# The opening of a fused attention and two-layer kernel: softmax sums of units 0 and 1 in column tiles, spread by transfers and multiplied by GpSimd

## The chip, the cores and the metric

The kernel runs on one core of a Trainium2 chip. The metric is the device time of one execution in microseconds (us). Before the change the median of three runs is 421.29 us (421.18 to 422.32). Engines are named as in the profile: PE is TensorE (matmuls; PEld are its weight loads), DVE is VectorE, ACT is ScalarE, POOL is GpSimd, SP is SyncE, which here only issues transfers. "L214" is line 214 of the kernel. Times of single events are counted from the start of the profiled span.

## The reference, cut to what matters

```python
def _attn_ref(q, k, v, g_q, g_k):             # q, k, v: (8, 12, 448, 64) float32
    q_n, k_n = rmsnorm(q, g_q), rmsnorm(k, g_k)
    scores = 1/sqrt(64) * q_n @ k_n.T
    attn = exp(scores - max(scores))           # rows of 448 keys
    attn = attn / (sum(attn) + 1e-09)
    return attn @ v

x = attention output as (3584, 768)
h = x @ moe_w_in                               # 768 x 2048
g = maximum(0.01 * h, h)
out = g @ moe_w_out                            # 2048 x 768
```

The kernel cuts the attention into 24 units: a unit is four heads of one batch, so a batch is three units. When the three units of a batch are done, the batch's x is complete and goes through the two weight matrices.

## The kernel before: the parts that the change touches

A unit has q and k as tiles of 128 partitions by 2 x 448 numbers. Its life is: square (`prep_sq` on ACT or `prep_sqp` on POOL), sum of squares (`prep_ssq`, DVE), inverse root (`prep_rinv`, ACT), normalise to f16 (`prep_norm`, DVE), transpose into `qkT` (PE plus a copy), scores in seven steps `qk` (PE), a row maximum for the shift (`shift_max`, `shift_mm`: DVE, PE, DVE), seven exponentials `ex` (ACT, one of 128x896 for each step), then the sums and the product with v.

There are two ways to form the sums and divide by them. The wide one is used by units 0 to 3 and the last one:

```python
def zsum(u, t0=0, t1=NS):                     # every sum stands 64 times: one row per row of the product
    for t in range(t0, t1):
        for r in range(2):
            for a in range(2):
                nc.tensor.matmul(s["zt"][r][64 * a:64 * a + 64, 0:S], ones16[64 * r:64 * r + 64],
                                 s["et"][64 * r:64 * r + 64, t, a], start=(t == 0), stop=(t == NS - 1))
def zinv(u):                                  # 1/z = exp(-ln z), read from PSUM
    s["rz"] = zpool.tile([P, 2, S], FP32, tag="rz", name="rz")
    nc.scalar.activation(s["rz"], s["zslot"][:, :, 0:S], AF.Ln)
    nc.scalar.activation(s["rz"], s["rz"], AF.Exp, bias=0.0, scale=-1.0)
def xmul(u):                                  # DVE multiplies the product in PSUM
    for r in range(2):
        nc.vector.tensor_tensor(xts[b][:, g, r], s["pv"][r][:, 0:S], s["rz"][:, r], op=ALU.mult)
```

The narrow one is used by units 4 to 22 (`narrow(u)` is `4 <= u < NU - 1`). The sums stand in four column tiles of 32 rows, only 224 columns wide; ACT takes the logarithm and the inverse of that small tile, and four transfers on the SP queue repeat it over the 128 partitions. The product is copied out of PSUM and multiplied from on-chip memory:

```python
def zcol(u):
    s["zc"] = aux([P, 512], FP32, "zc")
    for t in range(NS):
        for y in range(2):
            for a in range(2):
                c = 32 * (2 * y + a)
                nc.tensor.matmul(s["zc"][c:c + 32, 0:HS], onesr, s["et"][:, t, a, HS * y:HS * y + HS], ...)
def pv_out(u):
    s["x32"] = zpool.tile([P, 2, S], FP32, tag="x32", name="x32")
    nc.scalar.copy(s["x32"], s["pslot"][:, :, 0:S])
def zcol_ln(u):
    s["zs"] = zpool.tile([P, HS], FP32, tag="zs", name="zs")
    nc.scalar.activation(s["zs"], s["zc"][:, 0:HS], AF.Ln)
def zcol_inv(u):
    nc.scalar.activation(s["zs"], s["zs"], AF.Exp, bias=0.0, scale=-1.0)
    s["rz"] = zpool.tile([P, 2, S], FP32, tag="rz", name="rz")
    for r in range(2):
        for y in range(2):
            src = s["zs"][64 * y + r:64 * y + 64:2, None, :]
            nc.sync.dma_start(s["rz"][:, r, HS * y:HS * y + HS], src.broadcast_to([32, 4, HS]))
def xmul_pool(u, eng=nc.gpsimd):
    eng.tensor_tensor(xts[b][:, g], s["x32"], s["rz"], op=ALU.mult)
```

The pools that these tiles come from:

```python
raws  = tile_pool(name="raws",  bufs=3)      # q and k as loaded
zpool = tile_pool(name="zpool", bufs=1)      # x32, zs, rz: one buffer each, for all units
psum: tag "sT" bufs=2 (slot(), two banks each), tag "aux" bufs=4 (one bank each)
```

The weights come in on the POOL queue while the first units are at work: `load_w_in` is eight transfers, `load_w_out` two, and each v tile (`load_v`) one. q and k are loaded on the SP queue (`load`). [...] The end of the opening, up to the steady loop:

```python
ex(2)                                        # step 6 of unit 2
prep_rinv(4)
sums(2, 4, 5)
qk(3, STEPS[0])
sums(2, 5, NS)
zinv(2)                                      # unit 2 stays wide
shift_max(3)
xmul(2)
push(0)
first = slot()
moe1_part(0, first, 0, KT - 2)               # first matmuls of batch 0: parts 0, 1 of x are unit 0, parts 2, 3 unit 1
shift_mm(3)
ex(3)
moe1_part(0, first, KT - 2, KT - 1)          # part 4: unit 2
moe1_part(0, first, KT - 1, KT)              # part 5: unit 2
```

The `warm(n, bank)` calls are n matmuls whose result nobody reads; they keep PE active.

Of the kernel before, what the change touches and what calls it, by code (L numbers as in the profile page):

```python
# [8 lines left out]
FP32 = mybir.dt.float32  # L9
# [9 lines left out]
def kernel(  # L19
# [114 lines left out]
    def buf(u, name):  # L134
        if name not in st[u]:
            shape, dtype, bufs = SHAPES[name]
            st[u][name] = prep_p.tile(shape, dtype, tag=name[:2] if bufs == 3 and name != "qkT" else name, bufs=bufs, name=name)
        return st[u][name]
# [7 lines left out]
    def prep_sqp(u, tis=BOTH):  # L146
        for ti in tis:
            nc.gpsimd.tensor_tensor(buf(u, f"sq{ti}"), raw[u][ti], raw[u][ti], op=ALU.mult)
# [4 lines left out]
    def prep_ssq(u, c=ALL, tis=BOTH):  # L153
        for ti in tis:
            nc.vector.tensor_reduce(buf(u, "ssq")[:, ti, :, c[0]:c[1]], buf(u, f"sq{ti}")[:, :, c[0]:c[1]],  # L155
                                    axis=AXL.X, op=ALU.add)

    def prep_rinv(u, tis=BOTH):
        x = slice(tis[0], tis[-1] + 1)
        nc.scalar.activation(buf(u, "uu")[:, x], buf(u, "ssq")[:, x], AF.Ln, bias=eps_t, scale=1.0 / D)  # L160
        nc.scalar.activation(buf(u, "rinv")[:, x], buf(u, "uu")[:, x], AF.Exp, bias=0.0, scale=-0.5)  # L161
# [36 lines left out]
    def qk(u, steps):  # L198
        st[u]["sT"] = []
        for t in steps:  # L200
            sT = slot()
            score(u, t, (sT[:, 0], sT[:, 1]))
            st[u]["sT"].append((t, sT))

    def ex(u):
        s = st[u]
        if "et" not in s:
            s["et"] = epool.tile([P, NS, 2, S], FP16, tag="et", name="et")
        for t, sT in s["sT"]:
            if isinstance(sT, list):  # L210
                for a in range(2):
                    nc.scalar.activation(s["et"][:, t, a], sT[a][:, 0:S], AF.Exp, bias=s["eb"], scale=1.0)
            else:
                nc.scalar.activation(s["et"][:, t], sT[:, :, 0:S], AF.Exp, bias=s["eb"], scale=1.0)  # L214
# [6 lines left out]
    def shift_max(u):  # L221
        s = st[u]
        sT = s["sT"][0][1]
        if isinstance(sT, list):
            pm2 = small.tile([P, 2], FP32, tag="pm2", name="pm2")
            for a in range(2):
                nc.vector.tensor_reduce(pm2[:, a:a + 1], sT[a][:, 0:S], axis=AXL.X, op=ALU.max)
            s["spare"] = sT[0]
            nc.vector.tensor_reduce(s["spare"][:, 511:512], pm2, axis=AXL.X, op=ALU.max)
        else:  # L230
            s["spare"] = sT[:, 0]
            nc.vector.tensor_reduce(s["spare"][:, 511:512], sT[:, :, 0:S], axis=AXL.XY, op=ALU.max)  # L232
        s["dg"] = small.tile([P, P], FP16, tag="dg", name="dg")
        nc.vector.tensor_tensor(s["dg"], ident16, s["spare"][:, 511:512].broadcast_to([P, P]), op=ALU.mult)

    def shift_bank(u):
        st[u]["pb"] = aux([P, 512], FP32, "pb")

    def shift_mm(u):
        s = st[u]  # L240
        if u > 0 and "pslot" in st[u - 1]:
            pb = st[u - 1]["pslot"][:, :, S:S + 64]
            for x in range(2):
                nc.tensor.matmul(pb[:, x], onesp, s["dg"][:, 64 * x:64 * x + 64], start=True, stop=True)
            nc.vector.tensor_reduce(s["spare"][:, 510:511], pb, axis=AXL.XY, op=ALU.max)  # L245
        else:
            if "pb" not in s:
                shift_bank(u)
            pb = s["pb"]
            nc.tensor.matmul(pb[:, 0:P], onesp, s["dg"], start=True, stop=True)  # L250
            nc.vector.tensor_reduce(s["spare"][:, 510:511], pb[:, 0:P], axis=AXL.X, op=ALU.max)
        s["eb"] = small.tile([P, 1], FP32, tag="eb", name="eb")
        nc.vector.tensor_scalar(s["eb"], s["spare"][:, 510:511], -1.0, DELTA, op0=ALU.mult, op1=ALU.add)
# [14 lines left out]
    def zsum_slot(u):  # L268
        s = st[u]
        s["zslot"] = slot()  # L270
        s["zt"] = [s["zslot"][:, r] for r in range(2)]
        zsum(u)
# [19 lines left out]
    def pv_out(u):  # L292
        s = st[u]
        s["x32"] = zpool.tile([P, 2, S], FP32, tag="x32", name="x32")
        nc.scalar.copy(s["x32"], s["pslot"][:, :, 0:S])  # L295

    def zcol_ln(u):
        s = st[u]
# [23 lines left out]
    def zinv(u):  # L322
        s = st[u]
        s["rz"] = zpool.tile([P, 2, S], FP32, tag="rz", name="rz")
        if "zslot" in s:
            nc.scalar.activation(s["rz"], s["zslot"][:, :, 0:S], AF.Ln)
            nc.scalar.activation(s["rz"], s["rz"], AF.Exp, bias=0.0, scale=-1.0)
        else:
            for r in range(2):
                nc.scalar.activation(s["rz"][:, r], s["zt"][r][:, 0:S], AF.Ln)  # L330
                nc.scalar.activation(s["rz"][:, r], s["rz"][:, r], AF.Exp, bias=0.0, scale=-1.0)

    def pv(u, t0=0, t1=NS):
        s = st[u]
        if t0 == 0 and "pslot" not in s:
            s["pv"] = [aux([P, 512], FP32, "pv") for r in range(2)]
# [3 lines that stand above are left out]
                    nc.tensor.matmul(s["pv"][r][64 * a:64 * a + 64, 0:S], vts[u % NV][64 * r:64 * r + 64, a, t],  # L340
                                     s["et"][64 * r:64 * r + 64, t, a], start=(t == 0), stop=(t == NS - 1))

    def xmul(u):
        s = st[u]
        b, g = divmod(u, NQ)
        if b not in xts:
            xts[b] = xpool.tile([P, NQ, 2, S], FP16, tag="xt", name="xt")
        for r in range(2):
            nc.vector.tensor_tensor(xts[b][:, g, r], s["pv"][r][:, 0:S], s["rz"][:, r], op=ALU.mult)  # L349
            drop(s["pv"][r])  # L350
# [373 lines left out]
    def vcopy(dst, src, scaled=False):  # L724
        if scaled:
            nc.vector.tensor_scalar(dst, src, gcol, None, op0=ALU.mult)
        else:
            nc.vector.tensor_copy(dst, src)
# [11 lines left out]
    def warm(n, bank):  # L740
        for x in range(n):
            nc.tensor.matmul(bank[:, P:2 * P], onesp, onesp, start=True, stop=True)

    with tc.manual_schedule():
# [27 lines left out]
        def tr(u, ti, chunks, tp=None):  # L772
            if tp is None:
                tp = aux([P, NS, P], FP16, "tp")
            for c, copy in chunks:
                for x in range(*c):
                    nc.tensor.transpose(tp[:, x, :], buf(u, "n16")[:, ti, x].rearrange("p a d -> p (a d)"), ident16)
                copy(buf(u, "qkT")[:, ti, c[0]:c[1]], tp[:, c[0]:c[1]], ti == 0)
            return tp
# [21 lines left out]
        def trn(u, ti, copy):  # L801
            prep_tr(u, ti, ((ALL, copy),))
# [18 lines left out]
        warm(12, wb)  # L821
        qk(0, (2,))
        ex(0)
        warm(8, wb)
        qk(0, (3,))
        tr(1, 0, ((ALL, acopy),))
        tpk = tr(1, 1, ((K0, vcopy),))
        ex(0)
        qk(0, (4,))
        ex(0)  # L830
        tr(1, 1, ((K1, vcopy),), tpk)
        score0(1)
        shift_max(1)
        shift_bank(1)
        warm(10, st[1]["pb"])
        qk(0, (5,))
        ex(0)
        warm(8, st[1]["pb"])
        qk(0, (6,))
        ex(0)  # L840
        shift_mm(1)
        prep_ssq(2)
        ex(1)
        qk(1, (1,))
        ex(1)
        zsum_slot(0)
        pv(0)
        prep_rinv(2)
        zinv(0)
        prep_norm(2)  # L850
        gate(2)
        prep_sqp(3)
        load_v(3)
        load(5)
        prep_sqp(4, (0,))
        load_v(4)
        for f in range(2):
            load_w_out(8 * f, 8)
        qk(1, (2,))
        ex(1)  # L860
        trn(2, 0, vcopy)
        qk(1, (3,))
        ex(1)
        trn(2, 1, vcopy)
        xmul(0)
        qk(1, (4,))
        ex(1)
        qk(1, (5,))
        ex(1)
        score0(2)  # L870
        shift_max(2)
        qk(1, (6,))
        ex(1)
        shift_bank(2)
        warm(12, st[2]["pb"])
        shift_mm(2)
        prep_ssq(3)
        ex(2)
        qk(2, (1,))
        ex(2)  # L880
        zsum_slot(1)
        pv(1)
        prep_rinv(3)
        zinv(1)

        prep_norm(3)
        load(6)
        gate(3)
        prep_sqp(4, (1,))
        prep_sqp(5)  # L890
        load_v(5)
        qk(2, (2,))
        ex(2)
        trn(3, 0, vcopy)
        trn(3, 1, vcopy)
        xmul(1)
        prep_ssq(4)
        qk(2, (3,))
        ex(2)
        qk(2, (4,))  # L900
        ex(2)
        st[2]["zt"] = [aux([P, 512], FP32, "zt") for r in range(2)]
# [3 lines left out]
        sums(2, 3, 4)  # L906
        qk(2, (6,))
        ex(2)
        prep_rinv(4)
        sums(2, 4, 5)  # L910
        qk(3, STEPS[0])
        sums(2, 5, NS)
        zinv(2)
        shift_max(3)
        xmul(2)
        push(0)
# [129 lines left out]
```

## Time and profile before

| | before |
|---|---|
| time, median of 3 | 421.29 us |
| span of the profiled execution | 420.3 us |
| PE busy | 404.4 us (96%) |
| ACT busy | 303.6 us (72%) |
| DVE busy | 269.2 us (64%) |
| POOL busy | 83.0 us (20%) |
| moved by transfers | 62.42 MB |

How to read it: the page's first part gives each engine's busy time and share of the span. Its second part cuts the span into 40 slices of some 10.5 us, one digit each (9 is 90% busy or more); PEclk is the share of full clock speed that TensorE had, DMA the mean busy share of the 16 transfer engines. A timeline row is a start time, a duration, engine, line, the operation with written and read tiles, a count, and in brackets the idle time ahead of it with what ended that idle time. The stretch that the change rewrites is about 15 us to 46 us, the second to the fifth slice.

### The profile page before, as it was taken

The page shows a single profiled execution, that of the slowest core. Times are in us where ns is not written, and L with a number is a line of the kernel's source. Part 1 is how long each engine was busy: PE and PEld are TensorE (multiplying, and loading weights), DVE is VectorE, ACT ScalarE, POOL GpSimd, SP SyncE. Part 2 cuts the span into 40 slices and gives each one's busy share as a digit, 9 for nine tenths or more (in the row PEclk, how much of TensorE's full clock was granted, in tenths as well). Part 3 has the DMA queues.
Part 4 walks back from the last instruction along what each step waited for, and adds up shares of the span by engine and source line. Part 5 has one row for each costly group of instructions (what it writes and reads, how often), then busy time and mean ns, then how long its engine had stood idle before and what let it go on. Part 6 is the DMA issues. An engine that isn't in the chain of part 4 may idle for free.

```text
span 420.3 us, 9568 instructions
## 1 busy us (share of the span) xinstructions
PE 404.4 (96%) x3959; PEld 222.9 (53%) x3959; DVE 269.2 (64%) x440; ACT 303.6 (72%) x474; POOL 83.0 (20%) x75
## 2 busy tenths in 40 slices
PE   7977999999999999999999999999999999999995
PEld 6544444555445544555445544455445557558853
DVE  5788665787658736466448745467338787527762
ACT  5999878868987689867986779967986657653600
POOL 1958422300020111210121111120101101010000
PEclk9699999999999999999999999999999999999999
DMA  8999999889664795678565796578562460032023
GB/s 257 218 239 237 235 250 147 200 156 215 169 153 68 224 212 120 168 163 180 152 130 107 194 203 150 151 141 170 180 111 44 121 155 11 7 78 75 2 53 100
DMA packets 71951, 62.42 MB, mean 149 GB/s; under 512 B 36324, under 2 KB 67044, under 8 KB 71908
## 3 DMA queue, kind: packets, MB, share of 16 engines
q1 hardware_dynamic: 61312, 49.62, 47.2%
q0 software_dynamic: 10272, 11.80, 18.1%
q8 instruction: 31, 0.51, 0.5%
q10 hardware_dynamic: 324, 0.39, 0.3%
q14 instruction: 12, 0.10, 0.1%
HBM read 45.61 MB, written 11.01 MB: 135 GB/s over the span
## 4 chain that ended last, share of the span: by engine, by line
PE 83%; ACT 8%; DVE 6%; issue 1%; DMA 1%; SPq 0%; DVEq 0%; ACTq 0%
PE hps L362 27%; PE sT L195 8%; PE sT L340 6%; PE ma L444 5%; PE md L444 5%; PE mc L444 5%; ACT et L214 5%; PE bank L444 5%; PE bank L564 4%; PE op L403 3%; PE zc L283 3%; PE mb L444 3%; DVE n L167 2%; PE sT L444 2%; PE bank L403 1%
## 5 line engine op out<-in xcount | busy, mean ns | idle before, releaser
L214 ACT ACTIVATE et<-sT,eb 128x896 f16<-128x896 f32 x166 | 159.4, 1010 | 18.6 <-PE sT L195 16.9
L362 PE MATMUL hps<-xt,win 128*128 128x448 f16 x600 | 120.8, 353 | 0.2 <-DVE xt L349 0.2
L362 PEld LDWEIGHTS <-win 128*128 128x128 f16 x612 | 56.8, 98 | 58.2 <-issue 9.6
L320 POOL TENSOR_TENSOR xt<-x,rz 128x896 f16<-128x896 f32 x16 | 33.4, 2085 | 148.0 <-DMA rz<-zs 139.5
L356 ACT ACTIVATE gt<-hps 128x448 f16<-128x448 f32 x100 | 54.0, 556 | 6.1 <-PE hps L362 5.4
L167 DVE TENSOR_TENSOR n<-rq,rinv 128x896 f16<-128x896 f32 (+2 forms) x25 | 27.2, 1090 | 47.0 <-ACT rinv L161 44.2
L195 PE MATMUL sT<-qkT 64*64 64x448 f16 x664 | 53.2, 369 | 3.0 <-ACT et L214 1.9
L155 DVE TENSOR_REDUCE ssq<-sq 128x14 f32<-128x896 f32 (+2 forms) x49 | 50.3, 1058 | 1.6 <-ACT sq L144 1.6
L444 PEld LDWEIGHTS <-sa 128*128 128x128 f16 x352 | 32.8, 98 | 26.3 <-issue 6.1
L295 ACT COPY x<-sT 128x896 f32<-128x896 f32 x19 | 17.2, 906 | 36.4 <-DVE sT L245 36.4
L124 POOL DMA_DIRECT2D vt<-in_v_dram x24 | 18.2, 757 | 114.9 <-PE sT L340 107.4
L444 PEld LDWEIGHTS <-gt 128*128 128x128 f16 x264 | 25.2, 98 | 18.7 <-issue 2.1
L195 PEld LDWEIGHTS <-qkT 64*64 64x64 f16 x672 | 15.2, 105 | 36.8 <-issue 33.5
L340 PE MATMUL sT<-et,vt 64*64 64x448 f16 x532 | 28.5, 350 | 0.3
L403 PE MATMUL op<-wout,gt 128*128 128x384 f16 x160 | 28.4, 327 | 0.0
L232 DVE TENSOR_REDUCE sT<-sT 128x1 f32<-128x896 f32 x22 | 24.1, 1093 | 4.3 <-PE sT L195 4.3
L340 PEld LDWEIGHTS <-vt 64*64 64x64 f16 x672 | 20.7, 107 | 11.3 <-issue 1.7
L167 DVE TENSOR_TENSOR n<-rk,rinv 128x896 f16<-128x896 f32 (+2 forms) x26 | 26.1, 1009 | 0.0
L403 PEld LDWEIGHTS <-gt 128*128 128x128 f16 x192 | 17.6, 98 | 14.3 <-issue 3.0
L444 PE MATMUL ma<-wout,gt 128*128 128x384 f16 x128 | 23.5, 326 | 0.0
L425 DVE TENSOR_TENSOR sa<-gt 128x512 f16<-128x512 f16 (+1 forms) x15 | 8.2, 544 | 18.5 <-ACT gt L356 13.9
L144 ACT ACTIVATE sq<-rq 128x896 f32<-128x896 f32 (+2 forms) x18 | 16.3, 913 | 1.3 <-DMA rq<-in_q_dram 1.3
(135 smaller groups left out, 516.6 us busy)
## 6 DMA issues: line engine op xcount, KB each, us to landing
rq<-in_q_dram SPq DMA_DIRECT2D x24, 448.0 KB, 3.9
rk<-in_k_dram SPq DMA_DIRECT2D x24, 448.0 KB, 5.6
out_dram<-ost SPq DMA_DIRECT2D x52, 192.0 KB, 3.3
rz<-zs SPq DMA_DIRECT2D x76, 112.0 KB, 2.3
vt<-in_v_dram POOLq DMA_DIRECT2D x24, 224.0 KB, 5.1
win<-in_moe_w_in_dram POOLq DMA_DIRECT2D x8, 384.0 KB, 16.8
wout<-in_moe_w_out_dram POOLq DMA_DIRECT2D x2, 1536.0 KB, 29.7
out_dram<-ost SPq DMA_DIRECT2D x4, 96.0 KB, 2.1
```

What stands on the lines that cost most here:

```text
L124: nc.gpsimd.dma_start(vts[u % NV].rearrange("p a t d -> p a (t d)"), rows(v, u))
L155: nc.vector.tensor_reduce(buf(u, "ssq")[:, ti, :, c[0]:c[1]], buf(u, f"sq{ti}")[:, :, c[0]:c[1]], axis=AXL.X, op=ALU.add)
L167: nc.vector.tensor_tensor(buf(u, "n16")[:, ti, c[0]:c[1]].rearrange("p s a d -> p a s d"), src[:, :, c[0]:c[1]], buf(u, "rinv")[:, ti, :, ...
L195: nc.tensor.matmul(banks[a][64 * r:64 * r + 64, 0:S].rearrange("p (t x) -> p t x", t=NS), kT(u, r, a, t), qT(u, r, a), start=True, stop=True)
L214: nc.scalar.activation(s["et"][:, t], sT[:, :, 0:S], AF.Exp, bias=s["eb"], scale=1.0)
L232: nc.vector.tensor_reduce(s["spare"][:, 511:512], sT[:, :, 0:S], axis=AXL.XY, op=ALU.max)
L320: eng.tensor_tensor(xts[b][:, g], s["x32"], s["rz"], op=ALU.mult)
L340: nc.tensor.matmul(s["pv"][r][64 * a:64 * a + 64, 0:S], vts[u % NV][64 * r:64 * r + 64, a, t], s["et"][64 * r:64 * r + 64, t, a], start=(t ...
L356: nc.scalar.activation(dst, src, AF.Prelu, bias=0.0, scale=1.0, alpha=0.01)
L362: nc.tensor.matmul(hps[:, 0:S], win16[:, kt // 2, kt % 2, ts(ft, P)], xt[:, kt // 2, kt % 2], start=(kt == 0), stop=(kt == KT - 1))
L403: nc.tensor.matmul(op2[:, 0:HC], gt[:, ft, ds(col(t), P)], wout16[:, ft, ds(HC * half, HC)], start=(ft == 0), stop=(ft == FT - 1))
L444: nc.tensor.matmul(bank[:, 0:HC], a[:, f], b[:, f], start=(first and f == 0), stop=(f == HF - 1), skip_group_check=not first)
```

## The change

Units 0 and 1 take the narrow way instead of the wide one: `pv` and then `zcol` on PE, the product copied out of its two banks by ACT (a new `pv_out2`), the small tile inverted on ACT (`zcol_ln`, `zcol_inv`), four transfers, and the multiplication on POOL. Unit 2 stays wide. Around this, the order is edited: scores are issued ahead of the transposes of the next unit, the row maximum of units 1 and 2 is asked for earlier, the copies of unit 1's transposes all go to DVE, fewer `warm` matmuls are issued, the squares of unit 4 on POOL move to make room, and `prep_rinv(4)` goes behind `zinv(2)`. In the diff " ..." marks a cut, and some unchanged lines are drawn together. The aims that one reads from it are: less DVE and PE work in the opening, PSUM banks freed earlier (the wide sums held a two-bank slot), and scores ready before ACT asks for them.

```diff
+    def pv_out2(u):
+        s["x32"] = zpool.tile([P, 2, S], FP32, tag="x32", name="x32")
+        for r in range(2):
+            nc.scalar.copy(s["x32"][:, r], s["pv"][r][:, 0:S])
 ...
         qk(0, (2,))
         ex(0)
-        warm(8, wb)
+        warm(6, wb)
         qk(0, (3,))
-        tr(1, 0, ((ALL, acopy),))
+        tr(1, 0, ((ALL, vcopy),))
         tpk = tr(1, 1, ((K0, vcopy),))
         ex(0)
         qk(0, (4,))
         ex(0)
-        tr(1, 1, ((K1, vcopy),), tpk)
         score0(1)
         shift_max(1)
+        for x in range(*K1):
+            nc.tensor.transpose(tpk[:, x, :], ...)
         shift_bank(1)
-        warm(10, st[1]["pb"])
+        warm(6, st[1]["pb"])
         qk(0, (5,))
         ex(0)
-        warm(8, st[1]["pb"])
+        warm(6, st[1]["pb"])
         qk(0, (6,))
         ex(0)
         shift_mm(1)
+        vcopy(buf(1, "qkT")[:, 1, 1:NS], tpk[:, 1:NS])
         prep_ssq(2)
         ex(1); qk(1, (1,)); ex(1)
-        zsum_slot(0)
         pv(0)
+        zcol(0)
         prep_rinv(2)
-        zinv(0)
+        pv_out2(0)
+        zcol_ln(0)
+        zcol_inv(0)
         prep_norm(2)
         gate(2)
         prep_sqp(3)
         load_v(3)
         load(5)
-        prep_sqp(4, (0,))
+        xmul_pool(0)
         load_v(4)
         load_w_out (both halves)
         qk(1, (2,))
         ex(1)
-        trn(2, 0, vcopy)
         qk(1, (3,))
         ex(1)
+        trn(2, 0, vcopy)
         trn(2, 1, vcopy)
-        xmul(0)
         qk(1, (4,))
-        ex(1)
-        qk(1, (5,))
         ex(1)
         score0(2)
         shift_max(2)
+        qk(1, (5,))
+        ex(1)
+        shift_bank(2)
+        warm(8, st[2]["pb"])
         qk(1, (6,))
         ex(1)
-        shift_bank(2)
-        warm(12, st[2]["pb"])
         shift_mm(2)
         prep_ssq(3)
         ex(2); qk(2, (1,)); ex(2)
-        zsum_slot(1)
         pv(1)
+        zcol(1)
         prep_rinv(3)
-        zinv(1)
+        pv_out2(1)
+        zcol_ln(1)
+        zcol_inv(1)
         prep_norm(3)
         load(6)
         gate(3)
-        prep_sqp(4, (1,))
+        prep_sqp(4)
+        xmul_pool(1)
         prep_sqp(5)
         load_v(5)
         qk(2, (2,))
         ex(2)
+        qk(2, (3,))
+        ex(2)
         trn(3, 0, vcopy)
         trn(3, 1, vcopy)
-        xmul(1)
         prep_ssq(4)
-        qk(2, (3,))
-        ex(2)
         qk(2, (4,))
 ...
         ex(2)
-        prep_rinv(4)
         sums(2, 4, 5)
         qk(3, STEPS[0])
         sums(2, 5, NS)
         zinv(2)
+        prep_rinv(4)
         shift_max(3)
```

From `shift_max(3)` on, the two kernels have the same instructions in the same order.

More of the change, by code (lines that the diff above doesn't have):

```diff
@@ L295, in pv_out @@
         nc.scalar.copy(s["x32"], s["pslot"][:, :, 0:S])
+    def pv_out2(u):
+        s = st[u]
+        s["x32"] = zpool.tile([P, 2, S], FP32, tag="x32", name="x32")
+        for r in range(2):
+            nc.scalar.copy(s["x32"][:, r], s["pv"][r][:, 0:S])
     def zcol_ln(u):
@@ L830 @@
         ex(0)
-        tr(1, 1, ((K1, vcopy),), tpk)
         score0(1)
         shift_max(1)
+        for x in range(*K1):
+            nc.tensor.transpose(tpk[:, x, :], buf(1, "n16")[:, 1, x].rearrange("p a d -> p (a d)"), ident16)
         shift_bank(1)
-        warm(10, st[1]["pb"])
+        warm(6, st[1]["pb"])
         qk(0, (5,))
         ex(0)
-        warm(8, st[1]["pb"])
+        warm(6, st[1]["pb"])
         qk(0, (6,))
```

## The prediction

> **What bounds the kernel now.** I read the page first (busy shares, then the slices), then busy time by stage, then the timeline of ACT and PE through the opening, then the transfers.
>
> ```profile
> PE 404.4 (96%) x3959; PEld 222.9 (53%) x3959; DVE 269.2 (64%) x440; ACT 303.6 (72%) x474; POOL 83.0 (20%) x75
> ...
> PEclk9699999999999999999999999999999999999999
> DMA  8999999889664795678565796578562460032023
> ```
>
> PE bounds the whole, and from about 47 us on it leaves nothing over. So a change in the opening is worth exactly the shift of the moment at which PE enters its steady work, plus work taken from PE for good. The DMA row matters as much: the transfer engines are full in slices 1 to 6 and relax only in slices 7 to 11, while weights come in.
>
> The view by stage (from:to, length, busy time and count of each engine, clock, DMA share, GB/s):
>
> ```profile
> 20.00:30.00 10.00, 7.90 (x123) 4.85 (x121) 8.67 (x16) 9.94 (x15) 5.02 (x7) 1.00 1.15 244
> 30.00:41.00 11.00, 8.58 (x144) 4.73 (x143) 9.31 (x15) 9.40 (x13) 9.78 (x10) 1.00 1.12 234
> 41.00:47.00 6.00, 5.26 (x36) 2.60 (x36) 4.84 (x8) 4.82 (x11) 0.99 (x2) 1.00 1.18 229
> 47.00:60.00 13.00, 12.63 (x143) 6.45 (x142) 7.27 (x11) 10.95 (x18) 4.75 (x5) 1.00 1.14 243
> ```
>
> Columns after the length are PE, PEld, DVE, ACT, POOL. From 20 to 30 us ACT is full (9.94 of 10); from 30 to 41 us ACT, DVE and POOL are all near full; after 47 us PE is (12.63 of 13). The opening is a chain through ACT and DVE. The timeline shows its holes and its end:
>
> ```profile
> 24.24 0.90 ACT L326 ACTIVATE rz<-sT 128x896 f32<-128x896 f32 x1
> 25.17 0.95 ACT L327 ACTIVATE rz<-rz 128x896 f32<-128x896 f32 x1
> ...
> 31.22 1.16 ACT L212 ACTIVATE et<-s,eb 128x448 f16<-128x448 f32 x2 [0.61 <-DVE eb L253]
> ...
> 36.90 1.90 ACT L214 ACTIVATE et<-sT,eb 128x896 f16<-128x896 f32 x2 [0.43 <-PE sT L195]
> 39.29 1.90 ACT L214 ACTIVATE et<-sT,eb 128x896 f16<-128x896 f32 x2 [0.49 <-PE sT L195]
> ...
> 44.94 1.01 ACT L214 ACTIVATE et<-sT,eb 128x896 f16<-128x896 f32 x1 [1.09 <-DVE eb L253]
> ```
> ```profile
> 41.94 1.69 PE L370 MATMUL sT<-xt,win 128*128 128x448 f16 x8
> ...
> 44.56 0.54 PE L370 MATMUL sT<-xt,win 128*128 128x448 f16 x2 [0.50 <-DVE xt L349]
> ```
>
> ACT's holes before unit 3 add up to 1.53 us (0.61 + 0.43 + 0.49). PE starts batch 0's first matmuls at 41.94 and ends them at 45.10; the last two wait for unit 2's x. 45.10 us is the mark to compare with.
>
> **What the transfers cost in this stretch.** The transfers issued from 20 to 30 us (queue, size, us to landing), and then the spreading transfers of a later unit, 100 to 140 us:
>
> ```profile
> q0 software_dynamic: 1030, 1.43, 81.8%
> q1 hardware_dynamic: 585, 0.99, 32.4%
> ...
> rq<-in_q_dram SPq DMA_DIRECT2D x1, 448.0 KB, 9.8
> rk<-in_k_dram SPq DMA_DIRECT2D x1, 448.0 KB, 12.9
> ```
> ```profile
> rz<-zs SPq DMA_DIRECT2D x12, 112.0 KB, 2.3
> ```
>
> The same load that takes 3.9 us in the middle of the kernel takes 9.8 us here, because the weights' queue q0 holds the engines. The narrow way's 2.3 us is not what units 0 and 1 will see.
>
> [...] with 1030 packets of q0 beside 585 of q1 the load's landing grows 2.5 times. [...] Here the multiplication takes 2085 ns on POOL (L320, x16) against 1082 ns on DVE (L320, x3)[...]. [...] The trace has one such stretch, 11.5 to 18.4 us, after PE was busy under half of 8 to 10 us; the stage 12 to 20 us has a clock of 0.60.
>
> **The change part by part.**
>
> Work on PE: 28 `zsum` matmuls take 1.32 us (30.80 to the start of `pv` at 32.12), 28 `zcol` matmuls 0.85 us (131.49, a later unit). Two units save 0.9 us. Twelve warm matmuls fewer at about 0.06 to 0.12 us are some 1 us more, but PE has holes there, so little of that reaches the end.
>
> ACT per unit: removed 0.90 + 0.95 = 1.85. Added: two copies of 128x448 (no such row before; estimate 0.54 each, from Ln on 128x448 at 0.54 and the 128x896 copy at 0.91), Ln 0.36 and Exp 0.40: 1.84. No gain. The 1.01 us copy of unit 1's q transpose leaves ACT for DVE (0.68), but the scores of step 5 now stand behind unit 1's first scores, six transposes and six warm matmuls. Walking PE in order I get step 5 ready near 19.7 us and unit 1's first exponential at 21.6 against 21.79: gain 0.2.
>
> DVE: four `xmul` of 0.62, 2.5 us removed, 0.68 added. `shift_max(2)` no longer queues behind `xmul(0)` (1.15 us), so the 0.61 hole goes; unit 2's first exponential moves from 31.22 to about 30.75. Scores ahead of transposes close the 0.43 and 0.49 holes. If nothing else held, unit 2's sums would end about 1.3 us early.
>
> POOL, in its order: `gate(2)` at 26.5, two squares of 1.67 to 30.0, `load_v` 0.77, then `xmul_pool(0)` 2.1.
>
> Now the waits. `x32`, `zs` and `rz` have one buffer each. So ACT's copy of unit 1 waits until POOL has multiplied unit 0; and `zinv(2)`, unit 2's wide inverse, writes `rz` and so waits until POOL has multiplied unit 1. Both lie in ACT's order ahead of work that everything needs.
>
> - `zcol_inv(0)` ends about 26.05. Four transfers at 0.60 us of issue leave SP by 28.5, behind unit 4's load, whose k lands at 17.21 + 12.5 = 29.7.
> - They move 448 KB as 512 rows of 896 B (128 partitions each), as many rows as a q and k pair (2 x 256 rows of 1792 B), which takes 39.4 - 28.5 = 11 us here. If rows count, 7 to 8 us allowing for their half size; if bytes count, 5. Estimate: landing at 35 to 38. POOL multiplies until 37 to 40.
> - Unit 1's copy wanted to start at 33.4. It starts at 37 to 40; its small tile is ready 1.84 later, near 40.5.
> - SP's order puts unit 5's load behind the first four and ahead of the next four transfers. It now moves from about 36 to 44; unit 1's spread follows, 44 to 49 or 51. POOL's product ends at 51 to 53 (it was wanted at 41.9).
> - `zinv(2)` then runs: Ln 0.54, Exp 0.58, and DVE's 0.62 for the first half, 1.1 more for the second: +2.9; last matmuls 0.5: 54.5 to 56.5 against the mark 45.10. That is 9.5 to 11.5 us.
> - PE then stands idle from about 46 to 51[...].
>
> Sum: about +11 us, 421.3 + 11 = 432.
>
> **Rivals.**
>
> *Transfers hidden after all (landing 2.3 us).* Then POOL's order is the limit: `xmul_pool(0)` 30.8 to 32.9, v and two weight issues with their 0.9 wait to 36.4, gate, squares of unit 4 to 39.9, `xmul_pool(1)` to 42.0; `zinv(2)` ends 44.2 and the last matmuls end at 45.4 against 45.10. No gain either: about 421.5. For it: the reordering fits POOL's free places so well that 2.3 us seems assumed. Against it: the 9.8 and 12.9 us.
>
> *The engines' gain arrives (ACT and DVE ahead by 1.3 us, PE work down 0.9).* About 419.5 to 420. It needs `rz` free by 40 us, against POOL's 42.0.
>
> *Bytes, not rows, decide, and short rows slip between the long ones.* First landing near 33, second near 44: +3 to +5, about 425.
>
> **Range and chances.** I give the slow queue about 0.6 (429 to 438), the middle about 0.1 to 0.15, the hidden transfers 0.25 to 0.3 (420 to 423). 2% is 8.4 us, so slower than 429.7. A gain of 8.4 us has no source in a stretch whose holes add to 1.5 us. Predicted 432, range 420 to 438; faster 0.02, same 0.39, slower 0.59.
>
> **What the changed profile would show.** If right: ACT's second `pv_out2` copy idle for 3 us or more, released by POOL; POOL's two early products released by the DMA `rz<-zs`, whose landing is above 6 us; `zinv(2)`'s Ln idle, released by POOL `xt`; PE's first matmuls of batch 0 cut in two by a wait for POOL, ending near 55; a second dip of PEclk in the fifth or sixth slice. If the hidden-transfer rival is right: landings of 2 to 4 us, POOL never idle before a product, and the end of those matmuls within 0.5 us of 45.1. The prediction is wrong if the spread gets ahead of the weights' queue or of unit 5's load.

## The result and the profile after

The changed kernel takes 438.74 us, median of four runs (438.28 to 440.75), against 421.24 us for the kernel before, measured beside it (420.9 to 422.32). The ratio is 1.042, with a 95% interval of 1.0382 to 1.0458: 17.5 us longer.

The page of the kernel after, with the lines that answer to those of before (busy time of each engine, granted clock and transfer share in 40 slices):

```profile
PE 408.0 (94%) x3947; PEld 224.4 (51%) x3947; DVE 269.2 (62%) x437; ACT 303.1 (69%) x477; POOL 87.1 (20%) x77
...
PEclk9778879999999999999999999999999999999999
DMA  8998996188966488565964677757942461032013
```

ACT's busy time is unchanged within 0.5 us and DVE's is the same. POOL has 4.1 us more, its two products; PE has 3.6 us more with 12 matmuls fewer, at a mean granted clock of 0.972 against 0.992. The span grew by 15.9 us (420.3 to 436.2). So the engines hardly do more work; they wait. The clock stays below nine from the second slice to the sixth (7, 7, 8, 8, 7), where before only the second slice was low.

Busy time by stage of the kernel after, same stretches and columns as before (PE, PEld, DVE, ACT, POOL, then clock, transfer share, GB/s):

```profile
20.00:30.00 10.00, 8.42 (x111) 4.38 (x108) 6.89 (x11) 8.45 (x14) 3.86 (x5) 0.69 1.14 238
30.00:41.00 11.00, 4.52 (x84) 2.52 (x82) 6.07 (x10) 4.73 (x9) 3.51 (x4) 0.95 1.00 236
41.00:47.00 6.00, 4.61 (x51) 3.17 (x54) 2.06 (x3) 4.47 (x8) 5.61 (x6) 0.52 0.91 138
47.00:60.00 13.00, 6.39 (x50) 2.73 (x42) 4.47 (x8) 4.72 (x9) 6.04 (x4) 0.75 1.14 248
```

From 30 to 41 us ACT works 4.73 us where before it worked 9.40; from 47 to 60 us PE works 6.39 where before it worked 12.63, and part of that at half clock (0.50 from 54 to 60 us). What the engines wait for stands in the timeline of the kernel after (start, duration, engine, line, operation, idle time ahead and what ended it):

```profile
38.61 2.06 POOL L326 TENSOR_TENSOR xt<-x,rz 128x896 f16<-128x896 f32 x1 [7.49 <-DMA rz<-zs]
...
53.91 2.07 POOL L326 TENSOR_TENSOR xt<-x,rz 128x896 f16<-128x896 f32 x1 [7.30 <-DMA rz<-zs]
...
40.70 0.97 ACT L301 COPY x<-pv 128x448 f32<-128x448 f32 x2 [6.24 <-POOL xt L326]
...
56.02 0.54 ACT L336 ACTIVATE rz<-zt 128x448 f32<-128x448 f32 x1 [7.56 <-POOL xt L326]
...
49.20 0.55 PE L376 MATMUL sT<-xt,win 128*128 128x448 f16 x2
...
56.03 2.40 PE L376 MATMUL sT<-xt,win 128*128 128x448 f16 x6 [6.29 <-POOL xt L326]
...
58.33 1.70 PE L376 MATMUL sT<-xt,win 128*128 128x448 f16 x4
```

Read it as a chain. POOL waits 7.49 us for unit 0's spread. ACT, which must put unit 1's product into the one `x32` buffer, waits 6.24 us for POOL, and its next instruction, the logarithm of unit 1's small tile, starts at 41.56 us only. That tile is therefore late, its spread is late, and POOL waits 7.30 us again. ACT's `zinv(2)` waits 7.56 us for the one `rz` buffer, and PE's first matmuls of batch 0, cut in two, end at 60.03 instead of 45.10 us: 14.9 us late. The first store leaves at 97.28 us instead of 82.10, 15.2 us late, and the end of the span is 15.9 us late: the delay is made in the opening and nothing gives it back.

### The profile page after: what moved, and what is told of

Its sections match the earlier page's. It is cut to its first block, busy times and chain, and to the rows that moved or that the text cites. A ratio compares the mean times of both kernels' runs of the same rounds, so it can differ in the third digit from the quotient of the medians.

```text
span 436.2 us, 9566 instructions
## 1 busy us (share of the span) xinstructions
PE 408.0 (94%) x3947; PEld 224.4 (51%) x3947; DVE 269.2 (62%) x437; ACT 303.1 (69%) x477; POOL 87.1 (20%) x77
## 4 chain that ended last, share of the span: by engine, by line
PE 80%; DVE 5%; DMA 5%; ACT 5%; issue 2%; SPq 1%; POOL 1%; POOLq 0%; DVEq 0%; ACTq 0%
PE hps L368 26%; PE sT L195 8%; PE sT L346 5%; PE mc L450 5%; PE ma L450 5%; PE md L450 5%; PE bank L450 5%; PE bank L570 4%; DMA rz<-zs 4%; PE op L409 3%; PE zc L283 3%; ACT et L214 3%; PE mb L450 2%; DVE n L167 2%; PE sT L450 1%
## 5 line engine op out<-in xcount | busy, mean ns | idle before, releaser
L326 POOL TENSOR_TENSOR xt<-x,rz 128x896 f16<-128x896 f32 x18 | 37.5, 2085 | 165.9 <-DMA rz<-zs 165.9
L167 DVE TENSOR_TENSOR n<-rq,rinv 128x896 f16<-128x896 f32 (+2 forms) x25 | 28.4, 1139 | 46.4 <-ACT rinv L161 43.6
L283 PE MATMUL zc<-et,onesr 128*32 128x224 f16 x560 | 17.5, 265 | 0.0
```

Source lines behind the costliest of these rows:

```text
L167: nc.vector.tensor_tensor(buf(u, "n16")[:, ti, c[0]:c[1]].rearrange("p s a d -> p a s d"), src[:, :, c[0]:c[1]], buf(u, "rinv")[:, ti, :, ...
```

## The experiments

All times are medians; "excess" is the time above the kernel before measured in the same series, and the two product columns give the start of POOL's multiplications for units 0 and 1 in us (of its first half, where unit 1's is cut in two). "Mark" is the end of batch 0's first matmuls, 45.10 us in the kernel before. Product starts and marks are read from one profiled execution each, the excess from the medians, so the two need not agree to the microsecond (the profiled execution of `e3_own_buffers`, for one, is the slowest of its four, 432.9 us against a median of 430.92).

| kernel | product 0 | product 1 | mark | excess, us | ratio and 95% interval |
|---|---|---|---|---|---|
| the change | 38.61 | 53.91 | 60.03 | 17.5 | 1.042 (1.0382 to 1.0458) |
| e1_new_order_wide | on DVE | on DVE | 45.74 | 0.1 | 1.001 (0.9999 to 1.002) |
| e2_old_order_narrow | 37.09 | 52.58 | 58.57 | 16.0 | 1.0377 (1.0353 to 1.04) |
| e7_act_queue | 40.00 | 55.20 | 61.32 | 17.7 | 1.0428 (1.0408 to 1.0448) |
| e6_warm | 38.08 | 53.95 | 59.87 | 15.8 | 1.0367 (1.0337 to 1.0398) |
| e4_wout_late | 37.69 | 46.48 | 52.03 | 8.6 | 1.0204 (1.0187 to 1.0221) |
| e3_own_buffers | 38.28 | 46.97 | 54.44 | 9.1 | 1.0209 (1.0173 to 1.0244) |
| e12_both | 38.11 | 44.44 | 49.83 | 7.1 | 1.0169 (1.0135 to 1.0204) |
| e5_weights_late | 30.80 | 39.11 | 44.96 | 5.1 | 1.012 (1.0089 to 1.015) |
| e8_behind_squares | 31.37 | 40.16 | 45.72 | 8.3 | 1.0205 (1.0173 to 1.0236) |
| e10_squares_gated | 32.45 | 40.94 | 46.49 | 9.8 | 1.0217 (1.0195 to 1.0238) |
| e11_unit0_narrow | 32.24 | on DVE | 45.52 | 0.8 | 1.0019 (1.0009 to 1.0029) |
| e9_wide_warm | on DVE | on DVE | 44.78 | 0.4 | 1.002 (0.9999 to 1.004) |

The theory: the spreads land late because they share the transfer engines with the weights, and one buffer each of `x32`, `zs` and `rz` lets every late landing block ACT. There are three rivals: the new order, or the clock that it costs, is to blame; unit 5's load on the SP queue delays the second spread; or its place on SP's queue does, whatever stands ahead.

### The order alone, the narrow way alone

`e1_new_order_wide` is the changed kernel with wide sums and DVE products for units 0 and 1:

```diff
-        pv(0); zcol(0)
+        zsum_slot(0); pv(0)
-        pv_out2(0); zcol_ln(0); zcol_inv(0)
+        zinv(0)
-        xmul_pool(0)                # and xmul(0) behind trn(2, 1); unit 1 likewise
```

> The changed kernel with the narrow way undone: units 0 and 1 form wide sums and DVE multiplies, everything else of the new order stays (scores ahead, fewer warm matmuls, copies on DVE). If the late spreading transfers carry the whole loss, this is near the kernel before: 419.5 to 422.5 us. If the new order carries part of it (TensorE at half clock from 18 to 26 us, where the kernel before had full clock from 18.4), 423 to 426 us.

The time is that of the kernel before. The edited order does no harm in the total and brings nothing.

`e2_old_order_narrow` is the kernel before with the narrow way for units 0 and 1, and nothing else of the change:

```diff
-        zsum_slot(0); pv(0)
+        pv(0); zcol(0)
-        zinv(0)
+        pv_out2(0); zcol_ln(0); zcol_inv(0)
-        prep_sqp(4, (0,))           # xmul(0) goes too; unit 1 likewise, with prep_sqp(4) whole
+        xmul_pool(0)
```

> The kernel before with the narrow way alone for units 0 and 1, in the old order with all its warm matmuls. If the spreading transfers carry the loss: 435 to 439 us, with GpSimd's two products idle for over 6 us each, released by the transfers. If the new order carries it: 422 to 425 us.

16.0 of the 17.5 us are there; 1.5 us is left for the new order and the clock, and the two intervals overlap. POOL is idle 6.82 and 7.48 us ahead of its two products and ACT 6.21 and 7.38 us ahead of the copy and of `zinv(2)`, as in the changed kernel. The narrow way costs the time, not the order.

### Which transfers are in the way

`e4_wout_late` issues `load_w_out` behind unit 1's product:

```diff
-        for f in range(2): load_w_out(8 * f, 8)      # behind load_v(4)
         ...
         xmul_pool(1)
+        for f in range(2): load_w_out(8 * f, 8)
```

> The changed kernel with the two transfers of the second weight matrix issued behind GpSimd's product of unit 1 instead of ahead of it. If the weights' queue holds back the spread: the first spread is as before (landing near 38.6 us), the second, issued at 42.4 to 44.9 us, lands near 47 to 48 us instead of 53.9, batch 0's first matmuls end near 54 instead of 60.0, total 432 to 434 us. If unit 5's load on the same queue holds it back (my prediction's account), the second still lands near 53 us and the total stays at 437 to 439 us.

The second product starts at 46.48 instead of 53.91, although its spread leaves SP only 0.9 us earlier (41.50 against 42.41). The median landing of those four transfers fell from 8.6 to 3.3 us. The transfer view tells why. First the changed kernel, whose second spread is issued from 42.41 to 44.92 us: packets, MB and share of each queue from 42.0 to 46.5 us, then from 46.5 to 54.0 us. Weights and v are on q0; q, k and the spreads on q1.

```profile
q0 software_dynamic: 579, 0.70, 107.5%
q1 hardware_dynamic: 1, 0.00, 0.0%
...
q0 software_dynamic: 737, 1.12, 81.8%
q1 hardware_dynamic: 687, 0.66, 32.2%
```

Now the same view of `e4_wout_late`, 41.5 to 46.5 us:

```profile
q1 hardware_dynamic: 769, 0.79, 58.6%
q0 software_dynamic: 326, 0.27, 36.0%
```

In the changed kernel `w_out` is issued at 41.39 us on q0, one microsecond ahead of the spread on q1. From 42.4 to 46.5 us q1 moves nothing. Only then do the two queues share, 687 to 737. Without `w_out` there, q1 moves 769 packets in the five microseconds, the 512 of the spread and parts of two loads. Unit 5's load can't be what stood ahead in the changed kernel: its k had landed at 42.3 us (31.14 + 11.2). The kernel takes 430.23 us, less than the 432 to 434 expected.

The first spread stands still in the same way. It is issued from 27.45 us, and from 29 to 31 us the changed kernel's transfer view has one line only:

```profile
q0 software_dynamic: 227, 0.42, 113.5%
```

Its first packets come after 31 us, although the weights on q0, the second half of `w_in`, were issued as early as 18 to 23 us.

`e7_act_queue` issues the spreads of units 0 and 1 from ACT's queue instead of SP's:

```diff
-                nc.sync.dma_start(s["rz"][:, r, HS * y:HS * y + HS], ...)
+                (nc.scalar if u < 2 else nc.sync).dma_start(s["rz"][:, r, HS * y:HS * y + HS], ...)
```

> The changed kernel with the eight spreading transfers of units 0 and 1 issued from ACT, on ACT's own hardware queue, instead of SP's. If the place in SP's queue (behind and ahead of unit 5's load) holds the spread back: the second product of GpSimd starts 3 us or more earlier than 53.9 and the total is under 435 us. If the weights' software queue holds back every hardware queue alike: the two products start within 1.5 us of 38.6 and 53.9 us and the total is 437 to 441 us (the issuing costs ACT some 2.5 us per unit).

The landings are 6.9, 8.7 and 12.8 us (shortest, median, longest of eight), against 6.2, 8.0 and 9.4 in the changed kernel. POOL is idle 10.35 and 7.19 us ahead of its products, which start within the expected 1.5 us of those of the changed kernel. The place on SP's queue is not the cause, and ACT pays 2.9 us of issue for unit 0's spread besides.

`e5_weights_late` moves the second half of `w_in` behind unit 1's product too:

```diff
-        load_w_in(1024, 1024)
-        for f in range(2): load_w_out(8 * f, 8)
         ...
         xmul_pool(1)
+        load_w_in(1024, 1024)
+        for f in range(2): load_w_out(8 * f, 8)
```

> As the run before, and the second half of the first weight matrix goes behind unit 1's product too. If the weights' queue holds back the spread: the first spread lands by 31 to 33 us, the second by 41 us, the first matmuls of batch 0 end near 47 us, total 423 to 426 us, provided the weights then come in time. If the spread is slow by itself (short rows), landings stay over 6 us and the total is over 433 us.

The spreads land in 2.5, 3.2 and 4.8 us, POOL waits 1.07 and 0.68 us, and the mark is 44.96 us: 15.1 us earlier than in the changed kernel and level with the kernel before. That is the theory's main point shown: without the weights in that stretch the one-buffer waits shrink to 0.56 and 0.85 us on ACT. A q0 at work on a v tile did not hold a spread here: from 34.0 to 39.2 us q0 is at 38.4% and q1 at 45.7%, and the four transfers of the second spread, issued from 34.63 us, take 2.8 us (median). But the kernel is still 5.1 us longer than before, at 426.71 us just above the expected 423 to 426. The loss now lies behind the mark, in the timeline of `e5_weights_late`:

```profile
44.69 3.44 DVE L167 TENSOR_TENSOR n<-rq,rinv 128x896 f16<-128x896 f32 x1
48.06 2.56 DVE L167 TENSOR_TENSOR n<-rk,rinv 128x896 f16<-128x896 f32 x1
...
45.48 1.70 POOL L148 TENSOR_TENSOR sq<-rq 128x896 f32<-128x896 f32 x1
47.12 2.54 POOL L148 TENSOR_TENSOR sq<-rk 128x896 f32<-128x896 f32 x1
...
50.67 0.56 PE L175 MATMUL tp<-ident,n 128*128 128x128 f16 x7 [1.92 <-DVE n L167]
```

Unit 4's normalisation on DVE takes 3.44 and 2.56 us instead of 1.08 each, while unit 5's squares on POOL, which the weight issues pushed back, lie beside it. The author's reading is that they took turns. The four ends (47.18, 48.13, 49.66, 50.62) fit it: the gaps of 0.95, 1.53 and 0.96 us are about a normalisation (1.08), a square (1.68) and a normalisation. `e4_wout_late` has the same pattern (2.56 us for the second normalisation, 2.55 for the second square). That the first normalisation began 0.8 us before the first square and still ended after it stays unexplained. PE waits 2.4 us in all for `n`; by the first store the shift is 2.7 us (84.79 against 82.10).

`e8_behind_squares` tests that reading by issuing the same weights behind unit 5's squares:

```diff
         xmul_pool(1)
         prep_sqp(5)
+        load_w_in(1024, 1024)
+        for f in range(2): load_w_out(8 * f, 8)      # both gone from their old places
```

> As the run with both later weights behind unit 1's product, and the weights also go behind the squares of unit 5 on GpSimd. In that run DVE's two normalisations of unit 4 took 3.44 and 2.56 us instead of 1.08 each while GpSimd was squaring unit 5. If that overlap is the cause of its remaining loss, the two take under 1.2 us each here and the total is 420.5 to 423 us; if the weights then come too late, 424 to 428 us.

The normalisations take 1.09 and 1.08 us, though POOL issues the weights beside them (from 45.45 us), so the overlap with the squares was what stretched them; the mark is 45.72. What it was worth in the total is not shown, for the time is 430.16 us, above both expectations. The waits of PE from 40 to 60 us in `e8_behind_squares` (total, times, longest, in us) name the new place:

```profile
PE hps L368 <- DMA win<-in_moe_w_in_dram: 3.7, 2, 2.5
```

The second half of `w_in` now comes too late for the matmuls that read it, and the clock is 0.73 from 60 to 70 us, behind these two waits.

`e10_squares_gated` goes back to the places of `e5_weights_late` and instead moves the squares of unit 5 behind the gate that follows unit 4's normalisation:

```diff
-        prep_sqp(5)
         load_v(5)
         ...
                 prep_norm(4); gate(4)
+                prep_sqp(5)
```

> The narrow way for units 0 and 1 with the second half of the first weight matrix and the whole second one issued right behind unit 1's product, and the squares of unit 5 behind the gate of unit 4's normalisation. It should have both spreads landing in under 5 us, batch 0's first matmuls ending near 44.8 us, DVE's normalisations at 1.1 us, and the weights landing before 57 us: 420 to 422 us. If the later weights or the later squares give it back: 423 us or more.

Normalisations of 1.09 and 1.08 us again, mark 46.49, and no wait for `w_in`. The time is 431.83 us. The chain of work in `e10_squares_gated` has one piece that before has not (start, duration, what):

```profile
72.70 13.92 DMA qkT<-n
```

A transposing transfer, which takes 4.9 us in the kernel before from 60 to 90 us, took 13.92 here. `w_out` explains a part at most. It is in flight until about 75 us (longest landing 28.9 us); but the transfer ends at 86.62 us, over eleven microseconds later, and from 78 to 82.5 us all queues together move 13 to 92 GB/s only, against 201 to 294 from 60 to 77 us. In `e5_weights_late` two issued at 73.78 and 86.83 us, after `w_out` had landed, took 6.0 us (median). The cause stays open. PE is busy 4.93 of the 10 us from 80 to 90.

So moving the weights takes the loss out of the opening and puts it down elsewhere: beside POOL's squares, at PE's need of `w_in`, or at a later transfer.

### The buffers

`e3_own_buffers` leaves the weights where the change has them and gives unit 1's copied product and spread inverse buffers of their own, borrowed from the output tiles' pool, and the small tile a second buffer; POOL multiplies unit 1 in two halves, so that each half waits for its own spread only:

```diff
+        if u == 1: s["x2"] = [opool.tile([P, DM], FP32, tag="ost", name="x2") for r in range(2)]
+        if u == 1: s["r2"] = [opool.tile([P, DM], FP32, tag="ost", name="r2") for r in range(2)]
-        s["zs"] = zpool.tile([P, HS], FP32, tag="zs", name="zs")
+        s["zs"] = zpool.tile([P, HS], FP32, tag="zs", bufs=2, name="zs")
```

> The changed kernel with buffers of its own for unit 1's copied product, small tile and spread inverse, so that neither ACT's copy of unit 1 nor unit 2's wide inverse waits for GpSimd's earlier product (the spread and GpSimd's product stay; GpSimd multiplies unit 1 in two halves). If the one-buffer waits carry most of the loss: unit 1's four transfers are issued near 37 us instead of 42.4, ahead of the second weight matrix, GpSimd's second product starts at 45 to 48 us instead of 53.9, total 428 to 432 us. If the slow landing alone carries it: the second product still starts after 51 us and the total is 435 us or more.

ACT's copy no longer waits for POOL; unit 1's spread is issued from 35.28 us instead of 42.41. The excess falls from 17.5 to 9.1 us: the one-buffer waits carry about 8 us of it. The landings do not shrink: 7.5 to 10.4 us for unit 0, and 11.5 us (median) for unit 1, whose four take longer than in the changed kernel (median 8.6). So the rest is the late spread itself. PE's waits from 40 to 60 us in `e3_own_buffers`:

```profile
PE sT L387 <- POOL xt L335: 8.9, 2, 6.8
```

`e12_both` joins `e3_own_buffers` with the later `w_out` of `e4_wout_late`.

> Own buffers for unit 1 (as in the run with own buffers) together with the second weight matrix behind unit 1's product. Each alone took some 8 us off. If they are two ways to the same 8 us (both only let the second spread land earlier): 428 to 431 us. If they add, because the second spread is then both issued early (35 to 39 us) and free of the second matrix from 41 us on: its product starts by 44.5 us, batch 0's first matmuls end near 49 us, total 425 to 427 us.

The second product starts at 44.44 and the mark is 49.83 us, 4.7 behind the kernel before. The two cures, worth 8.4 us (buffers) and 8.9 us (`w_out`) alone, bring 10.4 together: they largely cure the same wait, as the total of 428.68 us says too. The product and the mark came almost as early as the other expectation had them, yet the time did not: by the end of the profiled span 6.1 us are lost, not 4.7. The first spread is untouched by either, for the product of unit 0 starts at about 38 us in all three. What holds it goes with the second half of `w_in`: that is all that `e5_weights_late` moves beyond `e4_wout_late`, and there it starts at 30.80 instead of 37.69.

### The clock

`e6_warm` restores the numbers of warm matmuls of the kernel before and adds 70 ahead of batch 0's first matmuls:

```diff
-        warm(6, wb)                 # and 6, 6, 8 in the later places
+        warm(8, wb)                 # 10, 8, 12
         first = slot()
+        warm(70, first[:, 0])
```

> The changed kernel with the warm matmul counts of the kernel before (8, 10, 8, 12) and 70 warm matmuls more ahead of batch 0's first matmuls, where TensorE idles. If the lost clock (half clock at 20 to 26 us and 54 to 60 us) carries 2 to 3 us of the loss: 435.5 to 437 us. If it is hidden behind the transfers: 438 to 439.5 us.

The clock from 19 to 26 us is 1.00 instead of 0.50 and `zcol_inv(0)` ends at 25.14 instead of 27.43 us. Yet the first product starts only 0.5 us earlier and the second at the same time (53.95); the mark moves by 0.2 us. The faster clock is hidden behind the transfers. It isn't even shown to come from the warm matmuls: `e4_wout_late` and `e7_act_queue`, which have the changed kernel's instructions up to there with its fewer warm ones, also have a clock of 1.00 from 19 to 26 us. From 9 to 14, 14 to 19 and 19 to 26 us the changed kernel has 1.00, 0.70 and 0.50, `e7_act_queue` 0.80, 0.86 and 1.00, and `e4_wout_late` 1.00 throughout; what sets this apart was not shown. The median, 437.69 us, lies between the two expectations. The medians differ by about 1 us, the excesses by 1.7, and the ranges touch (436.74 to 438.64 against 438.28 to 440.75), so the clock is worth between nothing and 2 us here.

`e9_wide_warm` is `e1_new_order_wide` with the warm matmuls of the kernel before.

> The new order with wide sums and DVE's product for units 0 and 1 (as in the first run), with the warm matmul counts of the kernel before. If fewer warm matmuls cost the new order its gain: 419.8 to 421 us, batch 0's first matmuls ending near 44.5 us. If the order is worth nothing: 421 to 422 us, as the first run.

The mark comes at 44.78 us, 0.3 before that of the kernel before and 1.0 before that of `e1_new_order_wide`. But this execution happens to have a clock of 1.00 from 9 to 33 us, where `e1_new_order_wide` has 0.50 from 14 to 19 us and the kernel before 0.56, so the microsecond can't be credited to the warm matmuls. The time is not shorter: 422.21 us.

### One unit instead of two

`e11_unit0_narrow` lets only unit 0 go the narrow way, with the second half of `w_in` behind its product, and two v tiles and `w_out` behind unit 5's squares:

```diff
         xmul_pool(0)
+        load_w_in(1024, 1024)
         ...
-        pv(1); zcol(1)
+        zsum_slot(1); pv(1)         # unit 1 as in the kernel before
         prep_sqp(5)
+        load_v(3); load_v(4)        # both gone from their old places, as load_w_out
+        for f in range(2): load_w_out(8 * f, 8)
```

> Only unit 0 takes the narrow way, with the second half of the first weight matrix behind its product; unit 1 stays wide; the second weight matrix goes behind the squares of unit 5. Landing of the one spread under 5 us, batch 0's first matmuls ending at 44.3 to 45.3 us, total 420 to 422 us; if GpSimd's later order or the later second matrix costs, 423 us or more.

The spread lands in 4.8 to 5.7 us (median 5.4), not quite under 5, POOL multiplies at 32.24, and the mark is 45.52 us. Nothing is gained either: 422.86 us, 1.0019 of before. None of the twelve beats the kernel before. The narrow way's best mark, 44.96 us, lies 0.14 us before that of the kernel before, less than the marks of the two wide runs differ by (44.78 and 45.74): no gain can be read from it.

## Why the prediction was right and where it was wrong

**The direction and the mechanism held.** It named the late landing under the weights' queue, ACT's copy of unit 1 waiting for POOL (3 us or more; it was 6.24), `zinv(2)` waiting for POOL (7.56), the first matmuls of batch 0 cut in two, a dip of the clock in the fifth or sixth slice (8 and 7 tenths) and nothing given back later. `e5_weights_late` and `e3_own_buffers` each take away one half of that mechanism: the delay at the mark goes in the first, and falls from 14.9 to 9.3 us in the second. The engine sums held too: ACT's narrow work for a unit is 0.97 + 0.36 + 0.39 = 1.72 us against the 1.84 reckoned, and POOL's product is 2.06 against 2.1.

**The size was short: 432 predicted, 438.74 measured, just above the range.** By the steps:

| step | predicted | measured |
|---|---|---|
| `zcol_inv(0)` ends | 26.05 | 27.43 |
| unit 0's spread has landed | 35 to 38 | 38.6 |
| ACT's copy of unit 1 | 37 to 40 | 40.70 |
| unit 1's spread has landed | 49 to 51 | 53.9 |
| `zinv(2)`, x and last matmuls behind the product | 3.4 | 4.05 |
| mark | 54.5 to 56.5 | 60.03 |

- **The step that failed is the second landing.** The prediction put unit 5's load ahead of it on SP's queue, moving until 44 us, and let the spread take 5 to 7 us from there. The load was already done, at 42.3 us. The spread was issued at 42.41 and stood still beside `w_out` until about 46.9 us, then took 7 us. So the upper estimate, by the number of rows, fits, and the start was wrong by 3 us, and for the wrong reason. `e4_wout_late` shows that it goes with `w_out`. Against the middle of the range this is 3.9 us, the largest term. The first landing has the same fault: it was put behind unit 4's load, which was nearly done at 27.45, and the spread stood still to 31 us; there the estimate of 35 to 38 nearly covered it.
- **The clock fell earlier than reckoned.** The prediction expected a second dip of the clock in the fifth or sixth slice only. In the profiled execution PE ran at 0.50 from 19 to 26 us; `pv(0)` took 2.83 us and `zcol(0)` 1.31, against 1.49 and 0.85 in `e7_act_queue` at a clock of 1.00, 1.8 us more and so all of the 1.4 us in the first row. By `e6_warm` it hardly counts in the end. The clock's other dip (0.50 from 54 to 60 us) makes the last row but one 0.6 us longer (the last four matmuls 1.70 us).
- **The gain of the order was overrated.** Where nothing else held, unit 2's sums were to end "about 1.3 us early". With wide sums the mark came 0.3 us early (`e9_wide_warm`) and 0.6 us late (`e1_new_order_wide`), in executions of different clock, and neither time is shorter than before.
- **Behind the mark** the prediction added nothing; the trace adds 1.0 us by the end of the span (14.9 to 15.9). Of the excess of 17.5 us the profiled pair shows 15.9. The remaining 1.6 us lies between single executions: the profiled one of the changed kernel (438.28 us) is 0.5 below its median, that of the kernel before (422.04) is 0.8 above its own, and 0.3 is time outside the spans.

So 11 became 17.5: 3.9 us at the mark (14.9 late instead of 11), 1.0 behind it, 1.6 between the profiled pair and the medians.

One reading of the prediction was wrong, without harm to the sum: it has the transfer engines full in slices 1 to 6 only, but the row that it shows stands at 8 or 9 through the tenth slice.

The rival of hidden transfers fell with landings of 6.2 to 9.4 us. Where the weights are away (`e5_weights_late`) the median landing is 3.2 us, and the mark is then that of the kernel before, within 0.2 us: without the late landings there is "no gain either" at the mark, as that rival reckoned. The rival of bytes (landings near 33 and 44 us, about 425) fell with 38.6 and 53.9: beside 737 packets of 1.12 MB on q0, q1 moved 687 of 0.66 MB, so the two shared by packets and not by bytes.

**Open:** why a spread on the hardware queue moves next to no packet for some four microseconds (1 from 42.0 to 46.5 us) while weights are in flight on the other queue, and only then moves beside it (687 packets to 737). The runs show that it isn't the order on the SP queue (`e7_act_queue`), that it goes with the weights (`e4_wout_late`, `e5_weights_late`) and that they need not have been issued just before it (the first spread); not what holds it. Nor is it settled how much of the late transpose in `e10_squares_gated` is `w_out`.

## What to carry to other kernels

Before a chain is led over transfers, take their landing time from the very stretch in which they'll run: 2.3 us in the steady part was 8.0 us in the opening, under the weights. Then ask what each late landing will hold: with one buffer ACT stopped at the first write to it, for 6.24 and 7.56 us, with all its later work, and a buffer of its own for unit 1 took away about half of the loss here. And when transfers are moved out of the way, follow them to their new place: three orders with late weights gave three different new losses.

## What the runs showed that was not expected

- With `w_out` issued one microsecond ahead, the hardware queue moved 1 packet in 4.5 us (42.0 to 46.5) while the software queue moved 579; then both went at 687 to 737.
- DVE's normalisation beside POOL's square: 3.44 and 2.56 us instead of 1.08, POOL's second square 2.54 instead of 1.68. With the squares behind the one-element `gate` copy (`e10_squares_gated`) the normalisations take 1.09 and 1.08 again.
- A transposing transfer landing after 13.92 us instead of 4.9.
- A half-clock stretch that differs between executions of the same instructions: 0.50 from 19 to 26 us in the changed kernel, 1.00 in `e4_wout_late` and `e7_act_queue`. There it made `pv(0)` and `zcol(0)` 1.8 us longer, so marks of single traces that differ by a microsecond prove little.
